# Three expert chunks of 256, 448 and 448 tokens for all blocks, in an attention, MoE and MLP kernel

## The chip, the cores and the metric

One core of a Trainium2 chip runs the whole program. The metric is the device time of one execution in microseconds; lower is better. TensorE is called PE here, VectorE DVE, ScalarE ACT, GpSimd POOL and SyncE SP.

## What is computed

Causal attention with a forget-gate decay (2 batches, 8 heads, 576 positions, head size 64) gives 1152 tokens of 512 features. A mixture of four experts follows, whose outputs are weighted by normalised domain probabilities and summed, then one MLP of hidden size 2048. From the reference:

```python
decay = cum[:, :, :, None] - cum[:, :, None, :]
scores = np.where(causal, -1000000000.0, scores + decay)
x = attn_out.transpose(0, 2, 1, 3).reshape(B * S, H * D)
for e in range(E):
    h = np.maximum(x @ w1[e], 0.0)
    out += p[:, e:e + 1] * (h @ w2[e])
h = x @ w_in
return (h * (1.0 / (1.0 + np.exp(-1.702 * h)))) @ w_out
```

## The kernel before

**Blocks and layers.** The two feed-forward parts are cut into 12 blocks of 512 hidden features: blocks 0 to 7 are halves of the four experts (NMOE = 8), blocks 8 to 11 quarters of the MLP. A block has two layers: `emit_l1` (x times a 512 x 512 weight) and `emit_l2` (hidden times a 512 x 512 weight, added into an accumulator). A layer of one chunk of tokens has four groups `g` of 128 output features; a group is 12 matmuls into one PSUM bank, since every product is made of three parts (high x high, low x high, high x low) with four slices of 128 features each. So a layer of a chunk is 48 matmuls of as many columns as the chunk has tokens.

**Chunks.** Attention makes its output in four chunks (`CH`, L20): per batch the first 256 positions and the other 320. Blocks 0 to 3 run on these four. Blocks 4 to 11 run on three wide chunks of 384 (`WN`, `WIDE`, L23 and L24). A wide chunk can cross the border between the batches, so `acc_parts` (L72) cuts its accumulator writes in two there.

**Order.** `visits` (L113) is the hand-written order of blocks and chunks; a visit loads and splits its weights once. Ten visits cover blocks 0 to 3, in pieces as attention's chunks become ready; eight visits cover blocks 4 to 11. `seq` (L124) puts layer 2 of a unit behind layer 1 of the next unit. `split_w` (L150) makes the high part of a weight tile on ACT (sometimes POOL) and the low part (`wlo`, L165) on DVE; `load_pair` (L138) issues the next 512 KB of expert weights from SP when a staging buffer is done with, four buffers in all.

**Attention as a generator.** `attention()` (L523) emits one stage step of one attention unit per pull: scores (L408), masks, exponentials, normalisation on POOL (L457), transposes (L475), the product with V (L505) and the split of the result into `xh` and `xl` (L514). Chunk 0 goes head by head without splitting; the others go in pairs of heads, whose keys and queries POOL prepares (L332 to L369). Chunks 2 and 3 share a pass. In the main loop (L729) `need` lists the places in `seq` where a chunk of attention must be ready, and before each one the loop pulls units at ceil(units due / groups left), at least one a group while any is due (L739 to L744). `drain` (L705) pulls whatever is still missing. The framework's scheduler then orders each engine's instructions by its own simulated times, so that matmuls of the blocks move into places where attention isn't ready.

**Evacuation.** Layer 1 of an expert block: ACT writes the rectified high part (L607), DVE the low part (L608). Layer 2: DVE multiplies by the token's probability (L639, or L636 into an empty accumulator) and POOL adds to the accumulator (L641). For the MLP: sigmoid on ACT, product on DVE, high part on ACT, low part on POOL (L611 to L616); layer 2 adds on DVE (L651) and the last block writes the output (L655, L656). PSUM has three banks for the blocks during attention (`ps_tile`, L97) and eight afterwards.

**After attention.** `begin_late` (L269) frees attention's memory for the MLP's converted weights: `mlp_convert` (L200) turns raw 64-bit weights into fp32 with seven DVE instructions for each of 32 tiles, paced by `cv_due` (L755). The probability rows (`dpb0`, `dpb1`, `load_dpb`) are broadcast loads from a small DRAM table.

Of the kernel before, what the change touches and what calls it, by code (L numbers as in the profile page):

```python
# [15 lines left out]
NT = B * S  # L16
# [6 lines left out]
WN = 384  # L23
WIDE = [NCH, NCH + 1, NCH + 2]  # L24
# [3 lines left out]
DPB1 = 576  # L28
# [5 lines left out]
def attn_moe_mlp(ctx: ExitStack, tc: tile.TileContext, qk0, qk1, qk2, v0, vp, fg, dp, wa_moe, wb_moe, wa_mlp, wb_mlp, outT):  # L34
# [37 lines left out]
    def acc_parts(c, g):  # L72

        t0, n = span[c]
        for b in range(B):
            a, z = max(t0, b * S), min(t0 + n, b * S + S)
            if a < z:
                yield slice(a - t0, z - t0), acc[b][:, g, a - b * S:z - b * S]
# [34 lines left out]
    visits = [(2, [0]), (1, [0]), (0, [0]), (3, [0, 1]), (0, [1]), (1, [1]), (2, [1, 2, 3]), (3, [2, 3]), (1, [2, 3]), (0, [2, 3])]  # L113
    visits += [(b, WIDE) for b in range(4, NBLK)]
# [124 lines left out]
    dpb = {1: dpb1}  # L239

    def dpb_of(e, c):
        t0, n = span[c]
        if e == 0:
            return (late["dpb0"] if CH[c][0] else dpb0)[:, CH[c][1]:CH[c][1] + n]
        return dpb[e][:, t0:t0 + n]

    def load_dpb(e, t):
        nc.sync.dma_start(out=t, in_=dpT[e:e + 1, :].to_broadcast([128, NT]))
        dpb[e] = t
# [19 lines left out]
    def begin_late():  # L269
# [25 lines left out]

    def load_plain(h0):
        G, wk = 4, SA
        if h0:
            a = acc[0].rearrange("p g s -> p (g s)")
            qd, kd = a[:, :G * wk], a[:, G * wk:2 * G * wk]  # L300
        else:
            qd, kd = (h_p.tile([128, 4 * WN], F32, tag=t, name=n)[:, :G * wk] for n, t in (("qd", "hh"), ("kd", "hl")))
# [264 lines left out]


    hbuf = {}

    def emit_l1(v_, b, c, g):
        n = span[c][1]
        if g == 0:
# [13 lines left out]
    def emit_first(k, last=False):  # L587
# [6 lines left out]
        for g in range(4):  # L594
            if k == 0:
                if g % 2 == 0:
                    p = ps_tile()
# [223 lines left out]
```

## Time and profile before

| | |
|---|---|
| Runs (3) | 730.58 us median, 730.52 to 731.89 |
| Profiled execution | 733.77 us, its span 732.0 us |
| Matmuls | 4488, of them 3840 in the two layers of the blocks |
| Span up to attention's last product with V | about 224 us |
| Granted TensorE clock, mean | 0.998 of 2.4 GHz |

The profiled execution is one run; its span goes from the first to the last instruction, and the rest of its time lies around the span. Durations below come from it. An engine's busy share counts instructions in flight; matmuls overlap, so the time that a stream of matmuls takes is read from the distance of their starts or from the chain of waits, not from the mean duration of one.

### The profile page before, as it was taken

The page shows a single profiled execution, that of the slowest core. Times are in us where ns is not written, and L with a number is a line of the kernel's source. Part 1 is how long each engine was busy: PE and PEld are TensorE (multiplying, and loading weights), DVE is VectorE, ACT ScalarE, POOL GpSimd, SP SyncE. Part 2 cuts the span into 40 slices and gives each one's busy share as a digit, 9 for nine tenths or more (in the row PEclk, how much of TensorE's full clock was granted, in tenths as well). Part 3 has the DMA queues.
Part 4 walks back from the last instruction along what each step waited for, and adds up shares of the span by engine and source line. Part 5 has one row for each costly group of instructions (what it writes and reads, how often), then busy time and mean ns, then how long its engine had stood idle before and what let it go on. Part 6 is the DMA issues. An engine that isn't in the chain of part 4 may idle for free.

```text
span 732.0 us, 11991 instructions
## 1 busy us (share of the span) xinstructions
PE 710.5 (97%) x4488; PEld 681.7 (93%) x4488; DVE 457.1 (62%) x1023; ACT 266.7 (36%) x629; POOL 295.1 (40%) x377
## 2 busy tenths in 40 slices
PE   4988999999999999999999999999999999999998
PEld 3577889999999999999998999999999999999997
DVE  4765767577748999999999542345962124424422
ACT  4445655566642233222221221223354433333320
POOL 5997896774422022332232432232462222222220
PEclk9999999999999999999999999999999999999999
DMA  8866744332125555454344200000100000000012
GB/s 269 248 194 210 213 162 137 118 103 87 59 90 193 154 193 160 162 173 117 114 144 115 87 30 30 1 1 1 58 0 1 1 1 1 1 0 1 1 44 86
DMA packets 31225, 68.81 MB, mean 94 GB/s; under 512 B 3224, under 2 KB 4768, under 8 KB 31168
## 3 DMA queue, kind: packets, MB, share of 16 engines
q1 hardware_dynamic: 31120, 68.01, 29.6%
q8 instruction: 35, 0.57, 0.3%
q14 instruction: 22, 0.18, 0.1%
q10 hardware_dynamic: 48, 0.05, 0.0%
HBM read 65.62 MB, written 2.41 MB: 93 GB/s over the span
## 4 chain that ended last, share of the span: by engine, by line
PE 84%; POOL 7%; DMA 5%; issue 2%; DVE 1%; SPq 1%; ACT 0%; POOLq 0%; DVEq 0%
PE m L625 39%; PE m L581 39%; PE s L408 2%; POOL e L457 2%; PE x L505 2%; DMA kq<-in_qk_dram 2%; PE t L475 2%; DMA qr<-in_qk_dram 2%; POOL klo L338 1%; POOL qlo L347 1%; POOL cb L360 1%; DMA kd<-fr 1%; POOL cb L363 1%; POOL khi L51 1%; POOL qhi L51 1%
## 5 line engine op out<-in xcount | busy, mean ns | idle before, releaser
L641 POOL TENSOR_TENSOR acc<-acc,tmp 128x384 f32<-128x384 f32 (+3 forms) x112 | 111.9, 1010 | 237.4 <-DVE tmp L639 237.0
L625 PE MATMUL m<-hh,wlo 128*128 128x384 f32 (+2 forms) x640 | 127.7, 320 | 0.9 <-DVE wlo L165 0.9
L625 PE MATMUL m<-hh,whi 128*128 128x384 f32 (+2 forms) x640 | 128.4, 320 | 0.0
L625 PE MATMUL m<-hl,whi 128*128 128x384 f32 (+2 forms) x640 | 128.3, 319 | 0.0
L581 PE MATMUL m<-xh,whi 128*128 128x384 f32 (+2 forms) x624 | 125.7, 321 | 2.2 <-POOL whi L51 2.2
L581 PE MATMUL m<-xh,wlo 128*128 128x384 f32 (+2 forms) x624 | 125.4, 321 | 0.0
L581 PE MATMUL m<-xl,whi 128*128 128x384 f32 (+2 forms) x624 | 125.1, 320 | 0.0
L54 ACT ACTIVATE whi<-wst 128x512 fp32r<-128x512 f32 x103 | 64.8, 630 | 117.6 <-PE m L581 65.9
L625 PEld LDWEIGHTS m<-hh,whi 128*128 128x128 f32 x640 | 106.0, 189 | 1.7 <-issue 0.8
L625 PEld LDWEIGHTS m<-hh,wlo 128*128 128x128 f32 x640 | 105.8, 189 | 1.7 <-DVE wlo L165 1.6
L581 PEld LDWEIGHTS m<-xh,whi 128*128 128x128 f32 x624 | 103.7, 188 | 3.2 <-POOL whi L51 2.5
L625 PEld LDWEIGHTS m<-hl,whi 128*128 128x128 f32 x640 | 106.2, 189 | 0.2
L165 DVE TENSOR_TENSOR wlo<-wst,whi 128x512 fp32r<-128x512 f32 x112 | 90.4, 810 | 25.1 <-ACT whi L54 12.6
L581 PEld LDWEIGHTS m<-xl,whi 128*128 128x128 f32 x624 | 104.0, 188 | 0.2
L581 PEld LDWEIGHTS m<-xh,wlo 128*128 128x128 f32 x624 | 103.8, 188 | 0.3 <-DVE wlo L165 0.2
L616 POOL TENSOR_TENSOR hl<-tmp,hh 128x384 fp32r<-128x384 f32 x48 | 49.1, 1025 | 133.2 <-ACT hh L54 133.2
L607 ACT ACTIVATE hh<-m 128x384 fp32r<-128x384 f32 (+2 forms) x112 | 48.8, 437 | 116.1 <-PE m L581 115.0
L608 DVE SCALAR_TENSOR_TENSOR hl<-m,hh 128x384 fp32r<-128x384 f32 (+2 forms) x112 | 54.8, 492 | 32.3 <-ACT hh L607 32.2
L639 DVE TENSOR_TENSOR tmp<-m,dpb 128x384 f32<-128x384 f32 (+2 forms) x80 | 40.8, 511 | 34.3 <-PE m L625 28.3
L614 DVE TENSOR_TENSOR tmp<-m,sg 128x384 f32<-128x384 f32 x48 | 26.6, 554 | 54.2 <-ACT sg L613 54.2
L448 ACT ACTIVATE e<-e,mx 128x128 f32<-128x128 f32 (+4 forms) x72 | 42.0, 584 | 43.1 <-DVE mx L434 39.3
L457 POOL TENSOR_SCALAR e<-e,sm 128x128 f32<-128x128 f32 (+4 forms) x72 | 46.1, 650 | 21.7 <-DVE sm L455 17.1
(93 smaller groups left out, 771.7 us busy)
## 6 DMA issues: line engine op xcount, KB each, us to landing
wst<-in_wa_moe_dram SPq DMA_DIRECT2D x28, 512.0 KB, 4.6
wst<-in_wb_moe_dram SPq DMA_DIRECT2D x28, 512.0 KB, 4.0
mst<-in_wa_mlp_dram SPq DMA_DIRECT2D x16, 512.0 KB, 3.5
mst<-in_wb_mlp_dram SPq DMA_DIRECT2D x16, 512.0 KB, 3.8
cb<-cumd SPq DMA_DIRECT2D x16, 256.0 KB, 6.1
qr<-in_qk_dram SPq DMA_DIRECT2D x12, 256.0 KB, 3.7
kq<-in_qk_dram SPq DMA_DIRECT2D x8, 352.0 KB, 7.0
vd<-in_vp_dram SPq DMA_DIRECT2D x8, 320.0 KB, 3.7
```

The source lines that it names most:

```text
L54: nc.scalar.activation(out=out, in_=in_, func=AF.Copy)
L165: sub = nc.vector.tensor_sub(lf, raw, f(hf))
L448: nc.scalar.activation(out=e[:, off:off + w], in_=e[:, off:off + w], func=AF.Exp, scale=-1.0, bias=mx, accum_out=sm[:, 0, k:k + 1])
L457: nc.gpsimd.tensor_scalar(out=e[:, off:off + w], in0=e[:, off:off + w], scalar1=sm[:, 0, i:i + 1], scalar2=1.0, op0=ALU.mult, op1=ALU.mult)
L581: nc.tensor.matmul(p[:, :n], lhsT=w[:, k, :], rhs=x[c][:, k, :], start=(j == 0 and k == 0), stop=(j == 2 and k == 3))
L607: nc.scalar.activation(out=hh[:, g, :n], in_=p[:, :n], func=AF.Relu)
L608: nc.vector.scalar_tensor_tensor(out=hl[:, g, :n], in0=p[:, :n], scalar=0.0, in1=f(hh[:, g, :n]), op0=ALU.max, op1=ALU.subtract)
L614: nc.vector.tensor_mul(t[:, :n], p[:, :n], s[:, :n])
L616: nc.gpsimd.tensor_sub(hl[:, g, :n], t[:, :n], f(hh[:, g, :n]))
L625: nc.tensor.matmul(p[:, :n], lhsT=w[:, k, :], rhs=x[:, k, :n], start=(j == 0 and k == 0), stop=(j == 2 and k == 3))
L639: nc.vector.tensor_mul(t[:, :n], p[:, :n], d)
L641: nc.gpsimd.tensor_add(a, a, t[:, z])
```

## The change

All twelve blocks run on the same three chunks: chunk 0 (the first 256 tokens, attention's first chunk) and two wide chunks of 448 (`WN`), tokens 256 to 703 and 704 to 1151. During attention the visits take chunk 0 alone through blocks 0 to 7, block after block. The visit of block 7 also takes the wide chunks; these then go back through blocks 6 to 0, for which the expert weights are loaded and split a second time. The MLP blocks take chunk 0 and the wide chunks in one visit each, the last block with chunk 0 at the end. `need` has two entries, both in the visit of block 7: the first wide chunk wants attention's chunk 2 ready, the second its chunk 3.

Two groups of a 256-token chunk share one PSUM bank (`bank_of`), and one evacuation instruction per engine handles both (512 columns); only the last layer of the last block keeps single banks. The accumulator is one tile for chunk 0 (`acc0`) and one for the other 896 tokens (`late["acc"]`), so evacuations aren't cut at the batch border. Probabilities of chunk 0 are kept for all four experts (`dpc`), those of the wide chunks are loaded for one expert at a time, two buffers. The first chunk's queries, keys and values lie in these tiles until they are needed. The conversion of MLP weights is paced at 1.1 steps a group before the MLP.

```diff
-WN = 384
-WIDE = [NCH, NCH + 1, NCH + 2]
+WN = 448
+WIDE = [NCH, NCH + 1]
...
-    dpb0 = const.tile([128, S], F32, name="dpb0")
-    dpb1 = const.tile([128, DPB1], F32, name="dpb1")
+    dpc = const.tile([128, 4, SA], F32, name="dpc")
     xh_t, xl_t = (big.tile([128, 4, NT], F32R, name=n) for n in ("xh", "xl"))
-    span = [(b * S + s0, n) for b, s0, n in CH] + [(i * WN, WN) for i in range(3)]
+    span = [(b * S + s0, n) for b, s0, n in CH] + [(SA + i * WN, WN) for i in range(2)]
...
-    acc = {0: big.tile([128, 4, S], F32, name="acc0")}
...
+    acc0 = big.tile([128, 4, SA], F32, name="acc0")
...
-    visits = [(2, [0]), (1, [0]), (0, [0]), (3, [0, 1]), (0, [1]), (1, [1]), (2, [1, 2, 3]), (3, [2, 3]), (1, [2, 3]), (0, [2, 3])]
-    visits += [(b, WIDE) for b in range(4, NBLK)]
+    order = list(range(NMOE))
+    visits = [(b, [0]) for b in order[:-1]] + [(order[-1], [0] + WIDE)]
+    visits += [(b, WIDE) for b in order[-2::-1]]
+    visits += [(b, [0] + WIDE) for b in range(NMOE, NBLK - 1)] + [(NBLK - 1, WIDE + [0])]
+    v_join, v_mlp0 = NMOE - 1, 2 * NMOE - 1
+    done_of = {0: v_join, WIDE[0]: v_mlp0 - 1, WIDE[1]: v_mlp0 - 1}
...
     def dpb_of(e, c):
+        if c == 0:
+            return dpc[:, e, :]
         t0, n = span[c]
...
+    def load_dpb(e):
+        dpb[e] = late["dp"].tile([128, NT - SA], F32, tag="dpb", name="dpb")
+        nc.sync.dma_start(out=dpb[e], in_=dpT[e:e + 1, SA:].to_broadcast([128, NT - SA]))
...
-        t = late["dpb0"] = late["rs"].tile([128, S], F32, name="dpb0b")
-        nc.sync.dma_start(out=t, in_=dpT[0:1, S:].to_broadcast([128, S]))
-        load_dpb(1, late["dp"].tile([128, NT], F32, tag="dpb", name="dpb"))
-        acc[1] = late["rs"].tile([128, 4, S], F32, name="acc1")
+        for b in (order[-1], order[-3]):
+            load_dpb(b // 2)
+        late["acc"] = late["rs"].tile([128, 4, NT - SA], F32, name="accw")
...
-            qd, kd = a[:, :G * wk], a[:, G * wk:2 * G * wk]
+            kd, qd, vd = acc0, dpc, hk[:, G * wk:]
         else:
...
+            vd = hq[:, G * wk:]
...
+        n = span[c][1]
+        if single or 2 * n > 512:
+            p = ps_tile()[:, :n]
+            return p, p, True, True
+        if g % 2 == 0:
+            banks[:] = [ps_tile()]
+        p = banks[0]
+        return p, p[:, n * (g % 2):n * (g % 2) + n], g % 2 == 0, g % 2 == 1
+    def evac_when(last, fn):
+        return fn if last else lambda: None
+    def of_group(t, c, g, p):
+        n = span[c][1]
+        k = p.shape[1] // n
+        return t[:, n * (g - k + 1):n * (g + 1)]
...
     def emit_l1(v_, b, c, g):
         n = span[c][1]
         if g == 0:
...
+        p, po, first, last = bank_of(c, g)
         whi, wlo = wa[v_, g]
-        p = ps_tile()
         for j, (w, x) in enumerate([(whi, xh), (wlo, xh), (whi, xl)]):
             for k in range(4):
-                nc.tensor.matmul(p[:, :n], lhsT=w[:, k, :], rhs=x[c][:, k, :], start=(j == 0 and k == 0),
-                                 stop=(j == 2 and k == 3))
-        return lambda: evac_l1(b, n, g, hh, hl, p)
+                nc.tensor.matmul(po, lhsT=w[:, k, :], rhs=x[c][:, k, :], start=(first and j == 0 and k == 0),
+                                 stop=(last and j == 2 and k == 3))
+        return evac_when(last, lambda: evac_l1(b, c, g, hh, hl, p))
...
-    def evac_l1(b, n, g, hh, hl, p):
+    def evac_l1(b, c, g, hh, hl, p):
+        hh, hl = of_group(hh, c, g, p), of_group(hl, c, g, p)
         if b < NMOE:
-            nc.scalar.activation(out=hh[:, g, :n], in_=p[:, :n], func=AF.Relu)
-            nc.vector.scalar_tensor_tensor(out=hl[:, g, :n], in0=p[:, :n], scalar=0.0, in1=f(hh[:, g, :n]),
-                                           op0=ALU.max, op1=ALU.subtract)
+            nc.scalar.activation(out=hh, in_=p, func=AF.Relu)
+            nc.vector.scalar_tensor_tensor(out=hl, in0=p, scalar=0.0, in1=f(hh), op0=ALU.max, op1=ALU.subtract)
...
+            w = p.shape[1]
+            s = late["t"].tile([128, 512], F32, tag="sg", name="sg")[:, :w]
+            t = tmp_p.tile([128, 512], F32, tag="tmp", name="tmp")[:, :w]
+            nc.scalar.activation(out=s, in_=p, func=AF.Sigmoid, scale=1.702)
+            nc.vector.tensor_mul(t, p, s)
+            round_act(hh, t)
+            nc.gpsimd.tensor_sub(hl, t, f(hh))
...
+        p, po, first, last = bank_of(c, g, b == NBLK - 1)
...
+        t0, n = span[c]
+        w = p.shape[1]
+        gs = slice(g + 1 - w // n, g + 1)
+        p = p.rearrange("p (g t) -> p g t", t=n)
+        a = acc0[:, gs, :] if c == 0 else late["acc"][:, gs, t0 - SA:t0 - SA + n]
+        tmp = lambda: tmp_p.tile([128, 512], F32, tag="tmp", name="tmp")[:, :w].rearrange("p (g t) -> p g t", t=n)
         if b < NMOE:
-            d = dpb_of(b // 2, c)
-            if c < NCH and first_of[c] == (v_, c):
-                for z, a in parts:
-                    nc.vector.tensor_mul(a, p[:, z], d[:, z])
+            d = dpb_of(b // 2, c).unsqueeze(1).to_broadcast([128, w // n, n])
+            if first_of[c] == (v_, c):
+                nc.vector.tensor_mul(a, p, d)
                 return
-            t = tmp_p.tile([128, WN], F32, tag="tmp", name="tmp")
-            nc.vector.tensor_mul(t[:, :n], p[:, :n], d)
-            for z, a in parts:
-                nc.gpsimd.tensor_add(a, a, t[:, z])
-            if b == NMOE - 1:
-                for z, a in parts:
-                    round_act(xh[c][:, g, z], a)
-                    nc.vector.tensor_sub(xl[c][:, g, z], a, f(xh[c][:, g, z]))
+            t = tmp()
+            nc.vector.tensor_mul(t, p, d)
+            nc.gpsimd.tensor_add(a, a, t)
+            if v_ == done_of[c]:
+                round_act(xh[c][:, gs, :], a)
+                nc.vector.tensor_sub(xl[c][:, gs, :], a, f(xh[c][:, gs, :]))
         elif b == NMOE:
-            for z, a in parts:
-                round_act(a, p[:, z])
+            round_act(a, p)
         elif b < NBLK - 1:
-            for z, a in parts:
-                nc.vector.tensor_add(a, p[:, z], a)
+            nc.vector.tensor_add(a, p, a)
         else:
-            t = tmp_p.tile([128, WN], F32, tag="tmp", name="tmp")
-            for z, a in parts:
-                nc.vector.tensor_add(t[:, z], p[:, z], a)
-            nc.sync.dma_start(out=outT[g * 128:(g + 1) * 128, t0:t0 + n], in_=t[:, :n])
+            t = tmp()
+            nc.vector.tensor_add(t, p, a)
+            nc.sync.dma_start(out=outT[g * 128:(g + 1) * 128, t0:t0 + n], in_=t[:, 0])
...
-    nc.sync.dma_start(out=dpb0, in_=dpT[0:1, :S].to_broadcast([128, S]))
-    nc.sync.dma_start(out=dpb1, in_=dpT[1:2, :DPB1].to_broadcast([128, DPB1]))
...
-    need = [(i, u[3]) for i, u in enumerate(seq) if u[0] == 1 and u[3] < NCH and first_of[u[3]] == (u[1], u[3])]
+    for e in range(4):
+        nc.sync.dma_start(out=dpc[:, e, :], in_=dpT[e:e + 1, :SA].to_broadcast([128, SA]))
+    wants = {0: 0, WIDE[0]: 2, WIDE[1]: 3}
+    need = [(i, wants[u[3]]) for i, u in enumerate(seq) if u[0] == 1 and u[1] == v_join and u[3]]
...
-            drain(c)
+        if kind == 1 and v_ <= v_join:
+            drain(wants[c])
...
-                cv_due[0] += 0.25 if v_ < 10 else 1.35 if b < NMOE else 1.5
+                cv_due[0] += 1.1 if b < NMOE else 1.5
...
-        if kind == 1 and (v_ == 8 and c == 2 or b == 5 and c == WIDE[0]):
-            load_dpb(3 if b == 5 else 2, late["dp"].tile([128, NT], F32, tag="dpb", name="dpb"))
+        if kind == 1 and c == WIDE[1] and v_ in (v_join + 2, v_join + 4):
+            load_dpb(visits[v_ + 2][0] // 2)
```

## Rows read from the trace of the kernel before

**Rows 1.** The page: busy time and share by engine; busy tenths in 40 slices; granted clock.

```profile
PE 710.5 (97%) x4488; PEld 681.7 (93%) x4488; DVE 457.1 (62%) x1023; ACT 266.7 (36%) x629; POOL 295.1 (40%) x377
...
POOL 5997896774422022332232432232462222222220
PEclk9999999999999999999999999999999999999999
```

**Rows 2.** The chain of waits: start us, us, engine, tile, line, matmuls merged.

```profile
96.80 1.79 POOL e L457 x2
...
102.68 1.17 POOL e L457
...
237.82 5.76 PE m L625 x48
...
249.34 7.04 PE m L625 x48
...
404.17 8.32 PE m L581 x48
```

**Rows 3.** Windows by stage: length, then PE, PEld, DVE, ACT, POOL busy, clock, DMA, GB/s.

```profile
60.00:104.00 44.00, 40.41 (x311) 35.20 (x312) 31.57 (x93) 24.85 (x66) 41.22 (x58) 1.00 0.63 196
104.00:126.00 22.00, 22.00 (x168) 20.11 (x169) 13.59 (x41) 10.58 (x31) 15.29 (x26) 1.00 0.38 123
126.00:204.00 78.00, 78.00 (x570) 71.53 (x569) 53.39 (x173) 48.12 (x133) 47.01 (x69) 1.00 0.30 99
224.00:400.00 176.00, 175.79 (x1183) 175.17 (x1182) 170.62 (x328) 44.67 (x89) 46.90 (x43) 1.00 0.49 152
```

**Rows 4.** Timeline of PE, score matmuls at 512 columns and what follows: start us, us.

```profile
51.20 0.40 PE L408 MATMUL s<-khi,qhi 128*128 128x512 f32 x1
...
51.90 0.64 PE L581 MATMUL m<-xh,whi 128*128 128x256 f32 x4
```

**Rows 5.** Windows of the lines L602, L581, L625 in that order, PE alone.

```profile
42.00:60.00 18.00, 5.81 (x44) 0.97 0.81 248
...
42.00:60.00 18.00, 5.37 (x36) 0.97 0.81 248
60.00:104.00 44.00, 8.59 (x60) 1.00 0.63 196
...
60.00:104.00 44.00, 12.91 (x90) 1.00 0.63 196
```

**Rows 6.** Timeline of PE: matmuls that began late, with what released them.

```profile
61.49 0.74 PE L581 MATMUL m<-xh,whi 128*128 128x256 f32 x4 [2.23 <-POOL whi L51]
...
402.51 0.97 PE L625 MATMUL m<-hh,wlo 128*128 128x384 f32 x4 [0.72 <-DVE wlo L165]
```

**Rows 7.** Groups by line and form: count, busy us and mean ns, idle before.

```profile
L165 DVE TENSOR_TENSOR wlo<-wst,whi 128x512 fp32r<-128x512 f32 x112 | 90.4, 810 | 25.1 <-ACT whi L54 12.6 <-POOL whi L51 11.7
...
L641 POOL TENSOR_TENSOR acc<-acc,tmp 128x384 f32<-128x384 f32 x32 | 39.9, 1255 | 77.9 <-DVE tmp L639 77.9
...
L639 DVE TENSOR_TENSOR tmp<-m,dpb 128x384 f32<-128x384 f32 x48 | 26.4, 552 | 28.8 <-PE m L625 26.1 <-POOL acc L641 2.2 <-POOL hl L616 0.4
...
L641 POOL TENSOR_TENSOR acc<-acc,tmp 128x256 f32<-128x256 f32 x24 | 21.4, 904 | 54.9 <-DVE tmp L639 54.8
...
L639 DVE TENSOR_TENSOR tmp<-m,dpb 128x256 f32<-128x256 f32 x16 | 6.7, 418 | 3.9 <-POOL acc L641 2.4 <-PE m L625 1.4
```

**Rows 8.** DMA issues of the expert weights: count, KB each, median us to landing.

```profile
wst<-in_wa_moe_dram SPq DMA_DIRECT2D x28, 512.0 KB, 4.6
```

**Rows 9.** Timelines of POOL and then of DVE beside each other near 393 us.

```profile
393.18 1.13 POOL L641 TENSOR_TENSOR acc<-acc,tmp 128x384 f32<-128x384 f32 x1 [10.16 <-DVE tmp L639]
...
393.35 1.51 DVE L165 TENSOR_TENSOR wlo<-wst,whi 128x512 fp32r<-128x512 f32 x1
```

**Rows 10.** Timeline of the end: last evacuation on DVE and last output issue.

```profile
728.69 0.56 DVE L655 TENSOR_TENSOR tmp<-m,acc 128x384 f32<-128x384 f32 x1 [1.53 <-PE m L625]
729.27 0.33 SPq L656 DMA_DIRECT2D out_dram<-tmp  x1
```

More of the change, by code (lines that the diff above doesn't have):

```diff
@@ L27 @@
 LEAD = 3
-DPB1 = 576
 NBLK = 12
@@ L294, in plain @@
         return c == 0
+    plain_h = [None, None]
     def load_plain(h0):
         G, wk = 4, SA
+        hq, hk = (h_p.tile([128, 4 * WN], F32, tag=t, name=n) for t, n in (("hh", "qd"), ("hl", "kd"))) if not h0 else plain_h
         if h0:
[L299 to L304 removed]
+            kd, qd, vd = acc0, dpc, hk[:, G * wk:]
+        else:
+            plain_h[:] = hq, hk
+            qd, kd = (t[:, :G * wk].rearrange("p (g s) -> p g s", g=G) for t in (hq, hk))
+            vd = hq[:, G * wk:]
+        vd = vd[:, :2 * G * D].rearrange("p (t g d) -> p t g d", t=2, g=G)
         for i, t in enumerate((kd, qd)):
@@ L569, in attn_moe_mlp, with bank_of @@
     hbuf = {}
+    banks = []
+    def bank_of(c, g, single=False):
+        n = span[c][1]
[12 more added lines that the diff above has]
+        return t[:, n * (g - k + 1):n * (g + 1)]
     def emit_l1(v_, b, c, g):
@@ L590, in emit_first @@
         if last:
-            hh, hl = hbuf[v_, c] = (h_p.tile([128, 4, WN], F32R, tag="hh", name="hh"),
-                                    h_p.tile([128, 4, WN], F32R, tag="hl", name="hl"))
-            return [lambda g=g: evac_l1(b, SA, g, hh, hl, first_p[g]) for g in range(4)]
+            hh, hl = hbuf[v_, c] = (h_p.tile([128, 4 * WN], F32R, tag="hh", name="hh"),
+                                    h_p.tile([128, 4 * WN], F32R, tag="hl", name="hl"))
+            return [evac_when(g % 2, lambda g=g: evac_l1(b, c, g, hh, hl, first_p[g // 2])) for g in range(4)]
         for g in range(4):
@@ L618, in emit_l2 @@
     def emit_l2(v_, b, c, g):
         n = span[c][1]
-        hh, hl = hbuf[v_, c]
+        hh, hl = (t[:, :4 * n].rearrange("p (k t) -> p k t", k=4) for t in hbuf[v_, c])
         whi, wlo = wb[v_, g]
-        p = ps_tile()
+        p, po, first, last = bank_of(c, g, b == NBLK - 1)
         for j, (w, x) in enumerate([(whi, hh), (wlo, hh), (whi, hl)]):
             for k in range(4):
-                nc.tensor.matmul(p[:, :n], lhsT=w[:, k, :], rhs=x[:, k, :n], start=(j == 0 and k == 0),
-                                 stop=(j == 2 and k == 3))
@@ L627, in emit_l2, with evac_l2 @@
-        return lambda: evac_l2(v_, b, n, c, g, p)
-    def evac_l2(v_, b, n, c, g, p):
-        t0 = span[c][0]
-        parts = list(acc_parts(c, g))
+                nc.tensor.matmul(po, lhsT=w[:, k, :], rhs=x[:, k, :], start=(first and j == 0 and k == 0),
+                                 stop=(last and j == 2 and k == 3))
+        return evac_when(last, lambda: evac_l2(v_, b, c, g, p))
+    def evac_l2(v_, b, c, g, p):
+        t0, n = span[c]
[4 more added lines that the diff above has]
+        tmp = lambda: tmp_p.tile([128, 512], F32, tag="tmp", name="tmp")[:, :w].rearrange("p (g t) -> p g t", t=n)
@@ L729, in attn_moe_mlp @@
     for i, (kind, v_, b, c) in enumerate(seq):
-        if kind == 1 and v_ < 10:
-            drain(c)
+        if kind == 1 and v_ <= v_join:
+            drain(wants[c])
         if not late and ready[0] == NCH - 1 and i >= need[-1][0]:
```

33 lines of the change are left out of this document (7 added, 26 removed).

## Prediction

> **What bounds the kernel now.** I read the page first: busy shares say which engine can set the end. TensorE's matmul row is busy 97% of the span, and its granted clock is 0.9 or more of the 2.4 GHz level in every slice; POOL is near full only in the first quarter [rows 1]. The chain of waits says which of the two ends last where. Until about 104 us it runs through POOL (attention's key and probability work), from there to the end through the matmuls of L581 and L625, nearly without a break [rows 2]. Stage windows confirm it: from 60 to 104 us POOL works 41.2 of 44 us, from 126 to 204 us PE 78 of 78 and POOL only 47 [rows 3]. So from 104 us on, time is the sum of matmul costs, and a matmul removed anywhere is time removed.
>
> That sum is easy to price. In the chain, 48 matmuls (one layer of one chunk) take 5.76, 7.04 and 8.32 us at 256, 320 and 384 columns [rows 2]: 120.0, 146.7 and 173.3 ns each. The three lie on one line: 0.4167 ns a column plus 13.3 ns a matmul. What a change of chunk widths can win is the 13.3.
>
> **Part 1: fewer, wider matmuls.** Before, blocks 0 to 3 run four chunks (256, 320, 256, 320), each with two layers: 2 x (2 x 5.76 + 2 x 7.04) = 51.20 us a block. Blocks 4 to 11 run three of 384: 6 x 8.32 = 49.92 us. Sum: 4 x 51.20 + 8 x 49.92 = 604.2 us, 3840 matmuls. After, every block runs 256, 448, 448. On the line 448 columns cost 0.4167 x 448 + 13.3 = 200.0 ns, a layer 9.60 us: 2 x 5.76 + 4 x 9.60 = 49.92 us a block, 599.0 us in all with 3456 matmuls. The difference is **5.1 us**, which is 384 matmuls x 13.3 ns; no column is saved. Blocks 4 to 11 gain nothing.
>
> No row shows 448 columns. The nearest wider ones are attention's score matmuls at 512: three start between 51.20 and 51.90 us [rows 4], 233 ns each where the line gives 226.7. Bounds for 448: the line (200.0; three rows within 0.1 ns of it, same code line) and halfway to the measured 512 (200.0 + 3.3 = 203.3). I take the line, since L581 and L625 themselves lie on it; the other end costs 2304 x 3.3 ns = 7.7 us and is a rival below.
>
> **Part 2: what attention is interleaved with.** Until all of chunk 3's attention is due, the old order offers 34.6 us (blocks 2, 1, 0, chunk 0) + 11.5 (block 3, chunk 0) + 4 x 14.08 (chunk 1) + 5.8 = 108.2 us of expert matmuls; the new one 8 x 11.52 + 9.6 = 101.8 us. That is 6.4 us less cover. The old PE had no gap there: between 104 and 224 us POOL was busy 47.0 of the 78 us in the middle [rows 3], so it has room, and the work moves behind attention. If the cover holds, cost 0.
>
> But the pace differs. The loop pulls attention units ahead of filler at one per group until those due are out. The old order stopped after chunk 1's 12 units and resumed 16 groups later; the new one has a single due time for chunks 1 and 2, so 29 units come in the first 29 groups of 256 columns. Up to 104 us nothing changes: by then 44 + 36 + 60 + 90 recorded filler matmuls had run [rows 5], 2.4 blocks of chunk 0, the same in both orders. After it, attention goes on at POOL's pace, instead of pausing. In 60 to 104 us, where POOL sets the pace, PE was idle 3.6 of 44 us [rows 3], part of it before a matmul released by POOL [rows 6]. Afterwards POOL was busy 15.3 + 47.0 = 62 us up to 204 us [rows 3]: that long its pace could set PE's. Bounds for the added idle: 0 (fillers run ahead wherever attention isn't ready, as they did) and 3.6/44 of those 62 us = 5.1 us. I take **+1.5**, nearer the lower end, since pass 2 has five units to a head pair's keys where pass 1 had three, so less POOL work a unit.
>
> **Part 3: weights twice.** Fillers before had 14 expert visits, now 15 (8 + 7): four more wst loads of 512 KB each, eight more splits. In the wide stretch a visit lasts 4 x 9.60 = 38.4 us, so they are covered by PE. Dense is the end of the attention phase, when visits are chunk 0 alone: 11.52 us for 2 MB, 182 GB/s; the core moved 196 GB/s in 60 to 104 us [rows 3], and a load lands in 4.6 us [rows 8]. SP's queue holds attention's loads among them, in order, as before. DVE does 8 wlo x 0.81 = 6.5 us a visit [rows 7] plus four evacuations of 512 columns, about 0.69 us each (from 418 ns at 256 and 552 at 384 [rows 7]): 9.3 of 11.5 us. Covered, with 2 us to spare. POOL adds at 512 wide are 1.6 to 1.7 us (from 904 and 1255 ns [rows 7]), two a layer in place of four of 0.9: same cost. Cost 0, upper end in the rivals.
>
> **Part 4: the small edits.** Paired PSUM banks halve evacuation instructions on DVE and ACT, which don't end last: 0. The evacuation starts one group (1.44 us) later, while L2 of a unit follows L1 of the next, 5.76 us: covered; if not, PE waits under 1 us a layer. The new accumulator and the two 896-column probability tiles come in when attention's memory is freed, and are needed one layer (9.6 us) later; the old ones were needed one layer (7.04 us) later. The MoE result of chunk 0 is complete long before the MLP, so MLP's first layer has no wait. Conversions keep running ahead on DVE, which was busy 171 of 176 us there [rows 3]; the one stall it caused, ending at 402.5 us (under 2 us in all [rows 6]), may go or move: 0, bounds -1.9 and +2. The tail: the last evacuation is 256 columns and the last output 128 KB in place of 384 and 192 KB. The old one took 0.56 us on DVE, then the output's issue at 729.27 and about 2.7 us to the end [rows 10]: 0.14 us on DVE and a little in the transfer, **-0.2**.
>
> **Sum.** -5.1 + 1.5 - 0.2 = **-3.8 us**: a span of 728.2 in place of 732.0. That run took 733.77 us, 1.77 around the span and 3.2 above the median of 730.58; the difference is taken from the median: **726.8 us**. Faster or slower means by over 0.2%, 1.5 us, about what a measurement here can tell.
>
> Beside that sum a page may be held. The Trainium skill ("TensorE: Matmul & The Clock Gate", Back-to-back issue gap) puts the gap of a warm matmul at N/2.4 + 2.5 ns, a fixed part of 2.5. By that, an estimate, 384 fewer matmuls are worth 1.0 us, not 5.1, and the sum would end at 730.9. The rows disagree: 120.0 ns at 256 columns where the rule gives 109.2, so it gets no chance.
>
> **Rivals.**
> *Attention crowds PE* (14%). POOL's pace is held through chunks 2 and 3 and PE idles 4 to 6 us more. For it: POOL's 94% in 60 to 104 us [rows 3]; against it: its 60% after 126 us. Gives -5.3 + 5 = 730.3, no difference.
>
> *Weight splits starve chunk 0* (12%; the one on the slower side). Place: the last four visits of chunk 0, once attention is out and conversions are pulled in. Price: a wlo beside a POOL add took 1.51 us, not 0.81 (the add started at 393.18 us, the wlo at 393.35 [rows 9]). If all did, DVE would need 8 x 1.51 + 2.8 = 14.9 us a visit of 11.5: 3.4 us each, 13.5 in four, 738.8 us; half of it gives 732. It decides from a mean wlo of (11.5 - 2.8) / 8 = 1.09 us. Against it: the mean over all is 0.81, and the same pace ran in the first three visits.
> The Trainium skill ("SBUF — State Buffer", Who interferes with whom) says that a DVE instruction with two SBUF inputs contends with a POOL instruction that reads SBUF. A wlo is such a one; the 1.51 us agrees.
>
> *448 columns lie off the line* (6%). 203.3 ns takes back 7.7 us: 730.58 - 3.8 + 7.7 = 734.5. It decides from 201.6 ns on, 3.8 us / 2304.
>
> *More than the sum* (8%): the early POOL waits and the 402 us stall shrink by 2 to 3 us: 722.5 to 724.
>
> **Chances.** The forecast, 724.5 to 729, has 60%. With the last rival, faster is 0.68; crowding gives 0.14 within 0.2%; the two slower ones 0.18. The range takes in the forecast, crowding and half of the starving: 723.3 to 732.5.
>
> **What the profile will show.** 3456 matmuls in L1 and L2; layers of 9.60 us x48 in the chain; PE idle between 60 and 210 us within 2 us of before; an end of attention some 5 us earlier; no wait of PE on wlo while chunk 0 runs alone. Wrong if 48 wide matmuls take over 9.7 us, or if the chain leaves PE for POOL or DVE after 110 us for more than 4 us.

## The result and the profile after

The changed kernel takes 741.32 us (median of four runs, 740.15 to 744.21), the kernel before beside it 730.52 to 731.89: a ratio of **1.0147 [1.0109, 1.0186]**, slower by 1.5%. A fourth run of the kernel before took 872.24 us and is left out, far outside all others. A second comparison on another chip gave 745.49 us and 1.0170 [1.0142, 1.0197]. The forecast was 726.8 us. By the medians the loss is 10.7 us. The profiled span is 739.4 us, only 7.4 longer than before, because the profiled run of the kernel before was itself 3.2 us over its median; the sums below explain these 7.4 us, and no profile shows where the other 3.2 lie. The page, its busy shares, POOL's tenths and the granted clock:

```profile
PE 717.5 (97%) x4104; PEld 652.9 (88%) x4104; DVE 456.2 (62%) x937; ACT 264.6 (36%) x577; POOL 285.4 (39%) x327
...
POOL 6987877784421003131233422313452122222221
PEclk9999989999999999999999999999999999999999
```

There are 384 matmuls fewer and as high a share, so PE still sets the end [rows 1]. One slice near 100 us has a lower clock. The windows of [rows 3] again (length, then PE, PEld, DVE, ACT, POOL busy, clock, DMA, GB/s):

```profile
60.00:104.00 44.00, 35.81 (x251) 30.86 (x251) 29.04 (x76) 22.39 (x58) 38.25 (x55) 0.94 0.61 188
104.00:126.00 22.00, 22.00 (x166) 19.75 (x166) 15.56 (x49) 13.46 (x37) 16.08 (x25) 0.96 0.40 129
126.00:204.00 78.00, 77.83 (x600) 69.40 (x599) 58.84 (x164) 51.32 (x132) 51.62 (x67) 1.00 0.38 117
224.00:400.00 176.00, 176.00 (x897) 162.46 (x897) 166.37 (x303) 42.32 (x76) 37.35 (x25) 1.00 0.43 137
```

From 60 to 104 us PE is idle 8.2 us instead of 3.6, and POOL is less busy too (38.25 for 41.22): POOL waits more. From 224 us on PE has no gap. The chain of waits (start us, us, what):

```profile
89.33 0.63 POOL whi L50
89.98 0.69 DVE wlo L160
90.74 0.59 DVE e L431
91.37 5.63 DMA cb<-cumd
97.17 0.91 issue
98.55 1.12 POOL e L454
99.71 1.12 PE t L472 x4
...
125.98 8.39 DMA cbs<-cumd
135.28 1.68 POOL klo L335
136.96 0.70 POOL e L454 x2
137.66 1.26 POOL acc L663
139.62 0.76 POOL qlo L344
140.38 0.91 POOL e L454
...
227.03 5.75 PE m L645 x48
232.78 9.73 PE m L600 x48
242.51 9.73 PE m L645 x48
```

A 256-column layer costs 5.75 us as before, but a layer of 448 columns **9.73 us, not 9.60**: 202.7 ns a matmul. Up to 104 us both chains run through POOL, but this one stands 5.63 us at a load of `cb` before POOL's `e` at 98.55 us, for which PE waits. Where the chain of before stays on PE from 104 us on [rows 2], this one also leaves it at 126 to 142 us, for a load of `cbs` and for POOL. That second detour cost PE nothing by itself in this profile: blocks' matmuls filled it, and from 126 to 204 us PE is idle 0.17 us in all.

To see how much is lost where, I sum for each profile by how much the distance from one matmul's start to the next exceeds the price of that matmul in an unbroken stream (119.7, 146.6, 173.4, 202.7 and 226.8 ns at 256, 320, 384, 448 and 512 columns of the blocks; 109 to 233 ns for attention's, of which only distances above the price count, as some start in pairs). This **excess** is PE's idle time and what a low clock costs it. Worked out from the traces, in us:

```
kernel              0-60 us  60-240 us  after 240   price of the blocks' matmuls
before                21.1      10.4       1.8       603.9
after                 20.1      19.1       0.3       604.8
after, second chip    17.7      24.4       1.0       604.8
```

Before to after: blocks' matmuls +0.9, excess up to 240 us +7.6 (39.1 for 31.6), after it -1.5, attention's own matmuls (the same in both, less close together) +1.7, the first matmul 1.0 earlier, and from the last matmul's start to the end 3.3 us for 3.7. That makes the 7.4 us within 0.1. Two profiles of the changed kernel, with the same order of instructions on every compute engine, differ by 5 us in the middle column on two chips, so between chips differences under that are no evidence. The kernel before has one profile.

In the first profile, one stall makes most of the added excess: 3.5 us from 95.9 to 99.7 us, where PE waits for POOL's `e`, and 2.8 us in the 6 us behind it, where the clock is at half. On the second chip that wait is 1.3 us, and others are longer: 3.5 us up to 64.6 us with a half clock until 70.2 us, and PE is idle 4.7 us from 104 to 204 us. So no single wait is the loss.

### The profile page after: what moved, and what is told of

Same layout as the page of the kernel before. It is cut to its first block, busy times and chain, and to the rows that moved or that the text cites. A ratio compares the mean times of both kernels' runs of the same rounds, so it can differ in the third digit from the quotient of the medians.

```text
span 739.4 us, 10990 instructions
## 1 busy us (share of the span) xinstructions
PE 717.5 (97%) x4104; PEld 652.9 (88%) x4104; DVE 456.2 (62%) x937; ACT 264.6 (36%) x577; POOL 285.4 (39%) x327
## 4 chain that ended last, share of the span: by engine, by line
PE 87%; POOL 7%; DMA 3%; issue 2%; DVE 1%; ACT 0%; POOLq 0%; DVEq 0%
PE m L645 40%; PE m L600 38%; PE s L405 4%; PE x L502 3%; PE t L472 2%; POOL e L454 2%; DMA cbs<-cumd 1%; POOL klo L335 1%; POOL qlo L344 1%; DMA cb<-cumd 1%; DMA kd<-fr 1%; POOL cb L357 1%; DMA kq<-in_qk_dram 1%; POOL cb L360 1%; POOL cbs L366 0%
## 5 line engine op out<-in xcount | busy, mean ns | idle before, releaser
L663 POOL TENSOR_TENSOR accw<-accw,tmp 128x448 f32<-128x448 f32 x56 | 80.2, 1437 | 223.6 <-DVE tmp L662 223.6
L645 PE MATMUL m<-hh,whi 128*128 128x448 f32 (+1 forms) x576 | 127.3, 340 | 0.0
L645 PE MATMUL m<-hl,whi 128*128 128x448 f32 (+1 forms) x576 | 127.2, 340 | 0.0
L645 PE MATMUL m<-hh,wlo 128*128 128x448 f32 (+1 forms) x576 | 126.3, 339 | 0.0
L600 PE MATMUL m<-xh,whi 128*128 128x448 f32 (+1 forms) x560 | 124.5, 341 | 0.0
L600 PE MATMUL m<-xl,whi 128*128 128x448 f32 (+1 forms) x560 | 124.0, 340 | 0.0
L600 PE MATMUL m<-xh,wlo 128*128 128x448 f32 (+1 forms) x560 | 122.7, 340 | 0.0
L600 PEld LDWEIGHTS m<-xh,whi 128*128 128x128 f32 x560 | 97.2, 189 | 6.5 <-DVE hl L628 0.3
L600 PEld LDWEIGHTS m<-xl,whi 128*128 128x128 f32 x560 | 97.1, 189 | 6.5 <-issue 0.4
L600 PEld LDWEIGHTS m<-xh,wlo 128*128 128x128 f32 x560 | 96.7, 189 | 6.3 <-issue 0.4
L636 POOL TENSOR_TENSOR hl<-tmp,hh 128x448 fp32r<-128x448 f32 (+1 forms) x40 | 47.5, 1191 | 137.8 <-ACT hh L53 137.8
L627 ACT ACTIVATE hh<-m 128x448 fp32r<-128x448 f32 (+1 forms) x80 | 43.7, 546 | 126.9 <-PE m L600 126.9
L628 DVE SCALAR_TENSOR_TENSOR hl<-m,hh 128x448 fp32r<-128x448 f32 (+1 forms) x80 | 50.4, 630 | 33.1 <-ACT hh L627 33.1
L662 DVE TENSOR_TENSOR tmp<-m,dpb 128x448 f32<-128x448 f32 x56 | 34.5, 618 | 27.9 <-PE m L645 25.6
```

The costliest lines, as they stand in the source:

```text
L600: nc.tensor.matmul(po, lhsT=w[:, k, :], rhs=x[c][:, k, :], start=(first and j == 0 and k == 0), stop=(last and j == 2 and k == 3))
L627: nc.scalar.activation(out=hh, in_=p, func=AF.Relu)
L628: nc.vector.scalar_tensor_tensor(out=hl, in0=p, scalar=0.0, in1=f(hh), op0=ALU.max, op1=ALU.subtract)
L636: nc.gpsimd.tensor_sub(hl, t, f(hh))
L645: nc.tensor.matmul(po, lhsT=w[:, k, :], rhs=x[:, k, :], start=(first and j == 0 and k == 0), stop=(last and j == 2 and k == 3))
L662: nc.vector.tensor_mul(t, p, d)
```

## The experiments

Each run had the kernel before beside it on the same chip, with medians of 733.1 to 734.2 us where the first comparison had 730.58. So runs of different comparisons are set side by side by their ratios, not by their times.

**Widths by themselves.** A kernel with only matmuls of L600's kind, 96 at each of eleven widths, no attention and no blocks (its output is zeros).

> The matmul price by itself: no attention, MoE or MLP, only eight groups of 12 matmuls at each of 11 widths from 256 to 512 columns, back to back with a new weight each and one ACT copy a group; the output is filled with zeros. If price is a line plus a rising part as the changed kernel's 9.73 us a layer says: 120, 147, 173 ns to 384, then 203 at 448 and 230 to 234 at 512. If 448 was dear only through what ran beside it: 200 at 448 and 227 at 512.

Timeline of PE in it (start us, us; four matmuls a row), the first and last rows of 384, of 448 with the next width's first, and of 512:

```profile
38.29 0.86 PE L83 MATMUL m<-xh,whi 128*128 128x384 f32 x4
...
54.24 0.85 PE L83 MATMUL m<-xl,whi 128*128 128x384 f32 x4
...
109.43 0.98 PE L83 MATMUL m<-xh,whi 128*128 128x448 f32 x4
...
128.89 1.00 PE L83 MATMUL m<-xh,whi 128*128 128x464 f32 x4
...
191.40 1.08 PE L83 MATMUL m<-xh,whi 128*128 128x512 f32 x4
...
212.26 1.07 PE L83 MATMUL m<-xl,whi 128*128 128x512 f32 x4
```

448: (128.89 - 109.43) / 96 = 202.7 ns. 512: (212.26 - 191.40) / 92 = 226.7. 384: (54.24 - 38.29) / 92 = 173.4. All widths, ns a matmul and what lies over columns x 0.4167 (256 without its first 24 matmuls, which came 212 to 228 ns apart):

```
256 120.0 13.3 | 320 146.7 13.4 | 384 173.4 13.4 | 400 183.1 16.4 | 416 187.9 14.6 | 432 196.6 16.6
448 202.7 16.1 | 464 210.5 17.2 | 480 215.0 15.0 | 496 225.6 18.9 | 512 226.8 13.4
```

So 448 is dear by itself, as the first expectation had it, but 512 lies on the line of 256, 320 and 384, as the second had it; all seven widths between 384 and 512 lie above that line.

**384 and 512 in place of 448 and 448.** Same counts of matmuls and loads.

```diff
-span = [...] + [(SA + i * WN, WN) for i in range(2)]
+span = [...] + [(SA, WN), (SA + WN, 512)]
-WN = 448
+WN = 384
-WF = 28
+WF = 22
```

> The changed kernel with the wide chunks at 384 and 512 columns instead of 448 and 448; same count of matmuls and of weight loads; the 512 chunk's hidden tiles come from a pool of its own, with 22 instead of 28 converted weights ahead. Width theory (448 is dear by itself, 512 is not): layers of 8.32 and 10.89 us in place of 2 x 9.73, 0.25 us less a pair of layers, 6.0 us less over 24 pairs: 735 us, ratio to before 1.004 to 1.008; attention's excess unchanged at 38 to 39.5. Rival (512 costs 233 ns as in attention's score matmuls, or the width of a chunk doesn't matter): layers of 8.32 and 11.2 us, 741 us, no difference to the changed kernel.

Measured: 741.08 us, ratio 1.0102 [1.0073, 1.0130], where the changed kernel beside it had 745.49: 4.4 us less. Its chain (start us, us, what):

```profile
231.36 5.75 PE m L647 x48
237.11 10.91 PE m L602 x48
248.02 8.34 PE m L647 x48
```

10.91 + 8.34 = 19.25 us for what took 2 x 9.73 = 19.46; with the 10.88 and 8.32 of other layers the blocks' matmuls fall from 604.8 to 598.8 us, the 6.0 expected. The other 1.6 us went into attention's part (excess up to 240 us 43.8 for 42.2). The ratio expected, 1.004 to 1.008, was missed, in part because it started from the 1.0147 of the first comparison and not from the 1.0170 beside this run. The price of the width is settled: it is 6.0 us of the miss.

**The pace of attention** (Part 2 of the prediction). Two kernels: the changed one with a due time for chunk 1 as in the old order (first edit), and the old one without its due time for chunk 1 (second edit).

```diff
 need = [...]
+need.insert(0, (7, 1))
```

```diff
 need = [...]
+need.pop(1)
```

> The changed kernel with a due place for attention's chunk 1 put back ahead of block 4, so that pulls stop after its 12 units and resume eight layers into the order. Theory 1 (pace): the extra PE idle of the attention phase (7.6 us by the distance of matmul starts) comes from pulling chunks 2 and 3 without that stop; then most of it goes and the time is 734 to 736 us. Theory 2 (schedule around evacuation and POOL's order): the loss lies before the stop, in the stall that ends at 99.7 us and the slow clock behind it; then the stall stays and the time is 740 to 742 us. Theory 3 (weight supply) sees no effect either. The layers of 448 columns take 9.73 us by all of them.

Measured: 740.22 us, ratio 1.0083 [1.0066, 1.0100], excess 18.0 up to 60 us and 20.1 from there to 240. The stall that ends at 99.7 us is gone (no wait of PE over 1.5 us between 70 and 200 us), but the excess is no less.

> The kernel before with its due place for chunk 1 taken out, so that its pulls run on as they do in the changed kernel; nothing else is changed. Theory 1 (pace): PE idles 4 to 7 us more in the attention phase and the time rises to 735 to 738 us. Theories 2 and 3: within 2 us of the kernel before.

Measured: 739.84 us, ratio 1.0091 [1.0065, 1.0118]. The time is as the pace theory wants, the place is not: the excess from 60 to 240 us is 11.6, as before, and it has 8.5 us after 240, in PE's waits there:

```profile
PE m L581 <- DVE hl L608: 3.1, 4, 1.5
PE m L625 <- DVE wlo L165: 2.2, 4, 0.9
```

In the profiles, then, the pace makes neither kernel idle in attention's part, and the theory fell as an account of where the time goes. The times leave something open. By ratio pause lies 0.6% under the changed kernel of the first comparison, about 5 us, which its profile (of its slowest run) doesn't show, and no run of the changed kernel stands on that chip to compare with.

**Paired banks.** The changed kernel with a bank for each group.

```diff
-        if single or 2 * n > 512:
+        if True:
```

> The changed kernel with one PSUM bank and one evacuation a group for chunk 0 again (256 columns each), except in the first unit's first layer. Theory 2 (schedule around paired evacuation): the stall that ends at 99.7 us goes and the time is 735 to 737 us. Theories 1 and 3: 740 to 742 us or a little more, since there are more instructions.

Measured: 742.47 us, ratio 1.0119 [1.0098, 1.0139], excess up to 240 us 38.4, where the changed kernel has 39.1 and 42.2. So the loss doesn't come from the pairing.

**POOL's share of the weight splits.** On the chain above, `whi` on POOL stands at 89.33 us behind an addition to `cbs`.

```diff
-(round_pool if v_ <= 2 and g == 3 else round_act)(hf, raw)
+round_act(hf, raw)
```

> The changed kernel with the high halves of the early weight splits made by ACT instead of POOL (all but those of the first visit's first weights). Order theory (the added idle of 60 to 110 us comes from POOL's queue: whi stands there behind a cbs addition that waits for its DMA, DVE's wlo waits for whi, the masks stand behind wlo on DVE, so the next cb load and with it POOL's e come late): DVE no longer waits 2.5 us and more for POOL, PE's wait of 3.6 us near 96 us falls below 1 us, excess by 240 us 33 to 35.5 instead of 39, time 4 to 6 us under the changed kernel beside it. Rival (the loads of cb and cbs themselves land late, whatever stands behind them): excess stays within 1.5 us of 39 and the time within 2 us.

Measured: 744.07 us, ratio 1.0152 [1.0111, 1.0193]; excess 24.1 from 60 to 240 us. POOL's waits on the `cbs` loads were 23.3 us between 50 and 200 us. The order theory in this form fell: with `whi` gone, `e` still stands behind the same addition (PE waits 14.3 us for `e` between 70 and 200 us). The same edit with 384 and 512 columns:

> Both edits together: widths 384 and 512, high halves on ACT. If both theories hold: 6.0 + 4 to 6 us less than the changed kernel, 729 to 731.5 us, within 0.3% of the kernel before. If only the width theory holds: 735. If only the order theory: 736 to 737.

Measured: 738.33 us, 1.0062 [1.0038, 1.0087], excess 24.4 from 60 to 240 us: the width's 6 us, nothing from `whi`'s place that the excess shows.

**Weight loads.** Between 50 and 200 us SP waits 63 us for `wlo` with a weight load (39 before), with attention's loads behind it. Both kernels without the weight loads of attention's visits; then the changed kernel with these loads issued again, but for only 16 of their 512 columns.

```diff
+if 0 < v_ <= v_join:
+    t = kept[kind, g]
+else:
+    t = kept[kind, g] = wst_p.tile(...)
     nc.sync.dma_start(out=t, ...)
```

> The changed kernel without the weight loads of visits 1 to 7: the first visit's raw weights stay in their four tiles and are split again for each of these blocks, so the expert part of the output uses block 0's weights there; every split, matmul and evacuation is still made. Queue theory (attention's loads of kq, qr, cb and cbs stand on SP behind weight loads that wait for DVE's wlo to free their tile, and share the transfer with them; weight loads come more often in the new order because each chunk-0 visit lasts only 11.52 us): SP's 60 us of waits on wlo between 50 and 200 us vanish, POOL's waits for cb and cbs fall from 15 to 23 us to under 8, PE's excess by 240 us falls from 38 to 42 to 28 to 34, time 5 to 10 us under the changed kernel. Rival (the loads are not what is late: the order of filler and attention, or DVE's load, makes the idle): excess stays over 37 and the time within 2 us of the changed kernel, ratio about 1.015.

Measured: 736.06 us, ratio 1.0032 [1.0009, 1.0056]; excess 17.1 up to 60 us, 17.4 to 240. The time fell as the queue theory wants; POOL's waits for `cb` and `cbs` did not (14.1 us, not under 8).

> The kernel before with the same edit for its visits 1 to 6 (block 2's raw weights reused there). Queue theory: before loses less, since its visits last up to 25.6 us: excess by 240 us from 31.6 to 28 to 31, time 1 to 3 us less. Rival: the same gain as in the changed kernel or none in both.

Measured: 736.59 us, ratio 1.0035 [1.0012, 1.0058]; excess 16.5 and **17.8**. Fewer loads, and more idle time from 60 us on than before: neither theory had that. Without the loads the two kernels take the same time, with about the same excess up to 240 us (34.5 and 34.3).

> As no_wst_loads, but each of the weight loads of visits 1 to 7 is issued again, in SP's queue and with the same wait for the split that frees its tile, for only 16 of the 512 columns: the expert part still uses block 0's weights, but for those columns. PE, POOL, DVE and ACT have the same instructions in the same order as in no_wst_loads. Queue theory (the waits in SP's queue hold attention's loads back): excess by 240 us rises from 34.5 to 38 or more, POOL's waits for cb and cbs from 14 to 17 us or more, time 3 to 6 us over no_wst_loads, ratio 1.008 or more. Bytes theory (the 2 MB a visit delay the other transfers): excess stays within 1 us of 34.5, ratio 1.002 to 1.005. Order theory (only the order of instructions moved the idle): the same as bytes.

Measured: 744.27 us, ratio 1.0128 [1.0100, 1.0155]. By time and by excess (42.8) that is what the queue theory expected: with the same order on every engine but SP, these loads and their waits cost 7 to 8 us. But they cost it in one place: excess 24.1 up to 60 us, where PE waits up to 4.6 us for a `whi`, and 18.7 from 60 to 240 us, 1.3 more than without loads. The changed kernel loses nothing up to 60 us (20.1 and 17.7 for before's 21.1), so this is not its loss; what the bytes of the full loads cost it stays open.

Two attempts at a cure: loads issued by ACT, and five raw tiles.

```diff
-nc.sync.dma_start(out=t, ...)
+(nc.sync if v_ == 0 else nc.scalar).dma_start(out=t, ...)
```

> The changed kernel with its weight loads from visit 1 on issued by ACT instead of SP; bytes and splits as they are. Queue theory: SP no longer waits for wlo; POOL's waits for cb and cbs fall under 12 us, excess by 240 us 33 to 37, time 3 to 7 us under the changed kernel, ratio 1.005 to 1.010; if ACT now waits for wlo, part of it comes back as PE's waits for ph or e. Bytes or order theory: no gain, excess 38 to 43, ratio 1.013 to 1.018.

Measured: 746.00 us, ratio 1.0164 [1.0116, 1.0211]; excess 22.9 and 20.9.

> wst_on_act with the chunks of 384 and 512 columns. Queue theory: 6 us under wst_on_act, ratio 0.997 to 1.002, about the kernel before or under it. Bytes or order theory: ratio 1.006 to 1.012, excess 38 to 45.

Measured: 741.91 us, 1.0101 [1.0074, 1.0128], excess 20.3 and 22.7.

> The changed kernel with chunks of 384 and 512 columns and five raw weight tiles instead of four (20 converted weights ahead instead of 22), so that a weight load no longer waits for the split made just before it. Queue theory: SP's waits on wlo fall by more than half, excess by 240 us from 43.8 (c384_512) to 33 to 38, time 5 to 9 us under c384_512: ratio to before 0.997 to 1.004, about the kernel before. Rival (only the number of bytes counts, or the loads are not the cause): excess stays over 41, ratio 1.008 to 1.012 as for c384_512.

Measured (`wst` with 5 buffers, WF 20): 744.72 us, ratio 1.0158 [1.0136, 1.0179]; excess 19.5 and 25.7, SP's waits on `wlo` 55 us. There is no gain in any of the three, as the rivals of the queue theory had it. In the last, SP's waits on `wlo` did not fall by half as expected (60.7 us in c384_512), so that run is no test of what they cost.

**The order alone.** Two steps left the order alone in which the framework's scheduler puts the instructions on the engines: the one from no_wst_loads to small_wst_loads, and the widths of 384 and 512, with which the order differs only from about 220 us on. There the excess from 60 to 240 us stays as well: the four pairs of kernels that differ in width, each on one chip, have 24.4 and 25, 24.1 and 24.4, 20.9 and 22.7, 20.2 (after_att_first, below) and 19.6. All other edits had also changed the order. The next one changes nothing else: in the traces each compute engine has the same instructions as before, in another order.

```diff
-        d = next(att, None)
+        with tc.high_priority(offset=150):
+            d = next(att, None)
```

> The kernel before with attention's instructions given an earlier place (by 150 instructions) when the order on the engines is chosen: same instructions and same data, another order on all queues. Order theory (the old kernel's 10.5 us of excess from 60 to 240 us are a property of its order, and any other order costs more): 15 us or more there, time 3 to 10 us over the kernel before, ratio 1.004 to 1.014. Work theory (the changed kernel's extra visits and its 29 units without a pause make the idle, whatever the order): stays within 3 us of 10.5, ratio within 0.4% of 1.

Measured on the kernel **before**: 749.46 us, ratio 1.0208 [1.0175, 1.0241]. The same instructions on the same data cost 16 us more. Its windows, as [rows 3]:

```profile
60.00:104.00 44.00, 37.72 (x266) 32.22 (x265) 23.38 (x73) 23.46 (x64) 32.14 (x50) 0.93 0.57 179
104.00:126.00 22.00, 20.03 (x147) 17.47 (x146) 14.00 (x49) 11.82 (x34) 17.68 (x27) 0.98 0.48 150
126.00:204.00 78.00, 75.10 (x552) 68.68 (x551) 48.79 (x167) 45.62 (x129) 45.17 (x73) 0.98 0.31 89
```

PE is idle 11.1 us up to 204 us where [rows 3] have 3.6. The excess from 60 to 240 us went from 10.4 to **25.5**, as much as in the worst variants of the changed kernel. Work theory fell here; order theory held, with more than the 3 to 10 us that it expected. So order alone can cost as much as the changed kernel lost.

> The changed kernel with the same earlier place for attention's instructions. Order theory: excess from 60 to 240 us moves by 4 us or more from the 19 to 24 it has, to either side; if it falls to 11 to 14, time falls by 6 to 10 us. Work theory: 17 to 26 again, ratio 1.012 to 1.019.

Measured: 747.27 us, ratio 1.0194 [1.0153, 1.0235]; excess 24.8 and 20.2. Here the middle column moved by less than two profiles of the changed kernel differ, not by the 4 us or more of order theory; the excess fits work theory, and the ratio lies just over its range.

> The same with the chunks of 384 and 512 columns: 6 us under after_att_first in both theories. Order theory with a fall of the excess: ratio 0.992 to 1.000, faster than before. Work theory: ratio 1.005 to 1.012.

Measured: 739.91 us, 1.0088 [1.0061, 1.0116], excess 24.2 and 19.6: the width's gain (7.4 us under after_att_first), and otherwise work theory's figures again. These two runs leave it open whether every order of the changed kernel is bad, or only those tried so far.

**One place in the order.** POOL's longest waits between 50 and 200 us (line, what it waited for: us in total, times, longest), in the reordered kernel before:

```profile
POOL cbs L369 <- DMA cbs<-cumd: 22.0, 6, 4.6
```

And the same view of the changed kernel with 384 and 512 columns:

```profile
POOL cbs L367 <- DMA cbs<-cumd: 18.1, 6, 5.4
```

The additions to `cbs` stand on POOL soon after their load is issued, and behind them stand `whi`, `klo` and `e`, for which DVE and PE wait. They are needed five to seven attention units later. The edit puts them one unit ahead of their use and holds them in program order.

```diff
-            nc.gpsimd.tensor_add(st["cbs"][z, 512:], st["cbs"][z, 512:], tri[z, z])
+            tc.keep_in_program_order(nc.gpsimd.tensor_add(...))
+            if i + 1 < len(seq) and not plain(seq[i + 1][0]) and seq[i + 1][1][1][0] == 512:
+                prep_cbs(*seq[i + 1])
```

> Chunks of 384 and 512 columns, and POOL's additions to cbs placed one attention unit before the unit that needs them instead of three before the pair's first. If POOL's waits for the cbs load are what the good order avoided: these waits fall from 13 to 23 us to under 6 us between 50 and 200 us, excess from 60 to 240 us from 25 to 11 to 17 us, time 8 to 14 us under c384_512, ratio to before 0.991 to 1.000. If they are only one of several places in the order: waits fall but e then waits for DVE or ACT, excess 17 to 23, ratio 1.003 to 1.008. If they cost nothing: excess 24 or more, ratio 1.008 to 1.013.

Measured: **729.13 us, ratio 0.9942 [0.9925, 0.9958]**, 4.0 us under the kernel before beside it, and by ratio under the changed kernel too. POOL's waits in it, in the same window:

```profile
POOL e L459 <- DVE sm L457: 10.3, 4, 4.4
POOL cbs L371 <- DMA cbs<-cumd: 6.6, 3, 4.3
```

The windows of its PE (length, busy, clock, DMA, GB/s):

```profile
60.00:110.00 50.00, 46.27 (x343) 0.97 0.62 189
110.00:240.00 130.00, 128.62 (x947) 1.00 0.40 123
```

Excess is 19.8 up to 60 us and 12.8 to 240, where c384_512 had 25; the blocks' matmuls take 598.8 us and the span 727.2. Each compute engine has the same instructions as in c384_512, so the changed kernel's work doesn't need the excess: another order of it has about as little as the kernel before.

That the waits for `cbs` are the reason is not shown. The same line of three other runs, the kernel before, after_att_first and before_no_wst in this order:

```profile
POOL cbs L369 <- DMA cbs<-cumd: 15.5, 6, 4.4
POOL cbs L366 <- DMA cbs<-cumd: 7.6, 4, 4.7
POOL cbs L372 <- DMA cbs<-cumd: 6.7, 3, 3.0
```

Their excess from 60 to 240 us is 10.4, 20.2 and 17.8: the kernel before has little excess with many of these waits, and the other two have much with as few as c384_512_cbs_late. The kernel before with this edit was not run, so whether it would gain as well is open.

## Why the prediction was wrong

**Part 1, the price of 448 columns: failed.** The 5.1 us needed 200.0 ns; it is 202.7. Over 2304 wide matmuls that is 6.2 us, and the blocks' matmuls cost 0.9 us more instead of 5.1 less. The line through 256, 320 and 384 was right, and so was the rival's price nearly (203.3). The weighting failed: the only wider row, attention's three matmuls at 512 [rows 4], was read as a bound that the blocks' own line outweighs. In a stream 512 is on the line, so that row said nothing of it, and nothing in the trace of before said whether a width between lies on it. Such a price deserved more than 6%, or the forecast the middle of the bounds. That the true price came out near the rival's is luck: the rival had it from the 233 ns of a row that says nothing of a stream. Its 734.5 us would not have been enough either. The Trainium skill ("TensorE: Matmul & The Clock Gate", Back-to-back issue gap) gives N/2.4 + 2.5 ns for an isolated warm matmul only, a fixed part of 2.5, and the prediction held it against a stream; these streams show 13.3 to 18.9, and the measurement decides.

**Part 2, the +1.5 us in attention's part: failed, in size and in mechanism.** Up to 240 us the excess grew by 7.6. "Up to 104 us nothing changes" is the sentence that broke: from 60 to 110 us the excess rose from 5.8 to 12.3, with chunk 0's blocks as filler in both. The rival of 14% had the size of PE's added idle time nearly right (4 to 6 us; 4.6 from 60 to 104 us), but by luck: it put it after 104 us and down to the pace, and the pace shows in neither profile as idle time of attention's part. What the prediction took as given is the order of instructions on the engines. before_att_first shows what that can cost by itself, 15 us of excess for the same work, and c384_512_cbs_late that the changed kernel's work can run with 12.8 in place of 25. Which place in the order makes the loss of the changed kernel stays open: c384_512_cbs_late moved other instructions too, and POOL's waits for `cbs` don't go with the excess from run to run.

**Part 3, weights twice: not refuted, its price open.** The splits don't starve chunk 0: `wlo` takes 840 ns on average, under the 1.09 us from which the starving rival decides, PE waits for none from 40 to 240 us, and after 240 us no wait is left. Without its weight loads the changed kernel was faster (1.0032 for 1.0147), but that edit changed the order too, so the loads' own price, put at 0, stays open.

**Part 4 and the tail: right.** The stall at 402 us [rows 6] is gone, and excess after 240 us is 0.3 for 1.8, inside the bounds of -1.9 and +2. The tail is 0.4 us shorter, where -0.2 was forecast.

**What would show it.** 3456 matmuls: yes. Layers of 9.60: no. Idle time from 60 to 210 us within 2 us of before: no. An end of attention 5 us earlier: no, its last matmul ends at 226.2 us, 2.5 later. No wait of PE on `wlo` while chunk 0 runs alone: yes. Both signs of a wrong forecast are there: 9.73 is over 9.7, and after 110 us the chain leaves PE for POOL for 5.3 us and for a load besides. The second sign was a poor one, since PE had no idle time there.

**The sum.** Part 1's -5.1 became +0.9, and Part 2's +1.5 became +7.6, with +1.7 from attention's matmuls and -1.0 from the first one, for which the prediction had no term. Part 4's 0 became -1.5 and the tail's -0.2 became -0.4. The idea behind the -5.1 was sound: with 384 and 512 columns the blocks' matmuls do cost 598.8 us, 5.1 under before, and with an order about as good as before's (excess 33.9 in all, for 33.4) the kernel is 4.0 us faster.

## What to carry to other kernels

Price a matmul width that no row shows from a run of that width alone; a line through other widths isn't enough. Where a scheduler orders the instructions, any edit can reorder all engines, and in the kernel before that alone was worth 16 us: compare excess by stage, and test the order by itself before explaining a loss by the work. An instruction that waits for a load is worth moving closer to its use; the one move tried here went with a gain of 12 us over c384_512, though its reason isn't settled.

## What the runs showed of the hardware

- Matmuls of this kind have no smooth price over columns: 480 cost 215.0 ns, but 496 cost 225.6, only 1.2 less than 512. Why is open.
- In the changed kernel PE is idle for 3.36 us up to 99.71 us, and the granted clock is at half, the 1.2 GHz level, from 98.8 to 105.6 us. The timeline of PE, and windows of PE (length, busy, clock, DMA, GB/s):

```profile
99.71 1.12 PE L472 MATMUL t<-identr,e 128*128 128x128 f32 x4 [3.36 <-POOL e L454]
...
99.00:105.50 6.50, 5.79 (x28) 0.50 0.40 124
106.00:110.00 4.00, 4.00 (x36) 1.00 0.01 4
```

In single_banks the same comes with an idle time of 4.28 us up to 63.06 us; in the kernel before the clock is at half from 39.8 to 43.2 us and then not again up to the last matmul. So this stall on POOL was paid for again in the matmuls behind it, with 2.8 us of excess. Not every stall is: in whi_on_act the clock stays at the upper level through an idle time of 3.22 us.
